# A constant deviation bound in place of a measured one, and pair differences on 32 rows, in a fused attention and MLP kernel

## The chip, the cores and the metric

The kernel runs on one core of a Trainium2 chip. The metric is the device time of one launch in microseconds (us); the time of a kernel is the median of its runs. The engines named are TensorE (PE, with its weight loads as PEld), VectorE (DVE), ScalarE (ACT), GpSimd (POOL) and SyncE (SP), whose queue issues the DMA transfers.

## The reference

Four batches of 12,480 rows of 128 numbers pass through two attention steps with 32 inducing points, and then through a two-layer MLP with a squared ReLU.

```python
x: (4, 12480, 128) float32, normal * 0.1      inducing: (32, 128) float32, normal * 0.1 * 2.776
w_in: (128, 2048), w_out: (2048, 128)

def mab(q, kv):
    s = scale * (q @ kv.transpose(0, 2, 1))
    s = s - s.max(-1, keepdims=True)
    a = np.exp(s)
    a /= a.sum(-1, keepdims=True) + 1e-09
    return a @ kv
h = mab(I, x)                  # 32 x 128 per batch
y = mab(x, h)                  # 12480 x 128 per batch
r = np.maximum(y @ w_in, 0.0)
out = (r * r) @ w_out
```

Each row of y is a weighted mean of the same 32 rows of h, with weights a that lie close to 1/32. The kernel uses this: y @ w_in is a @ (h @ w_in), so the MLP's first layer acts on 32 numbers in place of 128. Where a hidden column has one sign for all weights that can occur, its squared ReLU is zero or a plain square, and the sum over all such columns is a quadratic form in the 32 deviations d = 2^14 (a - 1/32). Only columns that may change sign are computed one by one; there is room for 16 of them per batch.

## The kernel before, in words

A batch has 26 chunks of 480 columns (4 groups of 120 rows). Chunks are grouped by four into 7 groups G. Four things are done for each batch.

`first(b)` (L238) computes the scores of the inducing points against x: it loads tiles `xp` (128 x 1920, nine buffers), multiplies (`scores`, L236), scales and takes the maximum on DVE (L254), exponentiates on ACT (L300), transposes on DVE (L310), and accumulates `hacc` on PE (L323) over blocks `xnb` of x (five buffers). It ends with `hT`, the 32 rows of h and their mean. `second(b, G)` multiplies the same xp tile with hT (freeing it), and forms the softmax over 32 in alternating steps on DVE, POOL and ACT. It writes the deviations as two fp16 halves, upper and lower, in the tile `a16`, to memory (`ad`, L389), and loads them back transposed as `dT` (L409): rows 0 to 31 the upper half, rows 32 to 63 the lower, rows 64 to 95 the upper again. `squares(b, G)` forms squares of the 16 single columns and of the mixed columns on PE, DVE and POOL, and puts them in rows 96 to 127 of dT. `prepare(b)` computes h @ w_in (`hwv`), decides which hidden columns are always off, always on or mixed, and makes the weights of the quadratic form: products `G` on DVE (L605), `wq` on PE (L611), then `w16` and `lin`.

For each chunk, `Chunk.up` makes two matmuls `hp` into two PSUM banks (L639), twice; their stationary operand `pairs` forms differences of two deviations, 512 of them in four blocks. `lift` squares two banks at once on ACT (L648). `down` sums four products with w16 and one with lin into `po` (L654, L655), which ACT or DVE scales (L658, L660), and SP stores.

Which columns count as mixed depends on rho, a bound on how far a weight can deviate from 1/32, relative to 1/32. Before the change it is measured: `largest(G)` (L290) takes the largest magnitude in every xp tile on DVE (`xm`, L292), `prepare` folds those with the spread of h (`dh`, L456 to L459), a matmul (L474) and a small row of two numbers, broadcast as `two` (L484).

```python
ts(row[:, 1:2], row[:, 1:2], 2 * scale * (1 + 2.0 ** -8), 2.0 ** -16, op0=ALU.mult, op1=ALU.add)
```

At the end `flags`, one number for each batch, tells whether the short way was allowed: rho small enough, at most 16 mixed columns, weights in range. If one is 0, the last part of the kernel (`every_column`) computes everything again by all 2,048 columns.

What runs beside what is fixed twice. The code interleaves the generators `first`, `prepare`, `second` and `squares` of the coming groups with the chunks (`background`, by counts of steps). The instructions so written are then put in an order for each engine by a simulated timeline, which uses its own estimates of durations and landings; an engine executes its own list strictly in order. A change of one instruction's cost can so move others. Besides, `held` sums expected work of ACT and DVE and gives some evacuations to the one with less.

Of the kernel before, what the change touches and what calls it, by code (L numbers as in the profile page):

```python
# [40 lines left out]
def attend_then_relu2_mlp(ctx: ExitStack, tc: tile.TileContext, xn, xT, indT, w_in, w_out, outT):  # L41
# [198 lines left out]
    def first(b):  # L240
# [49 lines left out]
        def largest(G):  # L290
            held["dve"] += 60 + 1.042 * 4 * WID[G]
            nc.vector.tensor_reduce(  # L292
                st.xm[:, G:G + 1], st.xp[G], axis=AX.X, op=ALU.max, apply_absolute_value=True,
            )

# [141 lines left out]
    def prepare(b):  # L437
# [37 lines left out]
        row = work.tile([1, 2], F32, tag="row", name=f"row_{b}")
        nc.vector.tensor_reduce(row[:, 0:1], ps[0:1, 0:P], axis=AX.X, op=ALU.max)
        nc.vector.tensor_reduce(row[:, 1:2], ps[0:1, P:P + MI], axis=AX.X, op=ALU.max)
        ts(row[:, 0:1], row[:, 0:1], 2.0 ** -60, None, op0=ALU.max)
        ts(row[:, 1:2], row[:, 1:2], 2 * scale * (1 + 2.0 ** -8), 2.0 ** -16, op0=ALU.mult, op1=ALU.add)
# [149 lines left out]
    class Chunk:  # L629
# [4 lines left out]
        def up(self, j):  # L634
            if j == 0:
                self.dT = self.st.aT[self.c // 4][:, :, (self.c % 4) * TP:(self.c % 4 + 1) * TP]
            hp = self.hp[j] = two_banks(f"hp_{self.b}_{self.c}_{j}")
            for i in range(2):
                nc.tensor.matmul(  # L639
                    hp[:, i, 0:CH].rearrange("p (q t) -> p q t", q=4), pairs[0:96, (2 * j + i) * P:(2 * j + i + 1) * P],  # L640
                    self.dT[0:96], start=True, stop=True,
                )
# [297 lines left out]
```

## Time and profile before

| | |
|---|---|
| three runs | 562.49, 556.12, 562.29 us; median 562.29 |
| profiled execution | 565.03 us, of which the span of instructions is 563.2 |
| granted TensorE clock, mean | 0.87 of full speed |
| DMA | 100.83 MB, mean 179 GB/s |
| first square of a chunk (ACT L648) | 96.3 us |
| first squares of batches 1, 2, 3 | 223.5, 350.7, 470.3 us |

The profile is read from several views: the busy time of each engine; the same cut into stages, with the columns PE, PEld, DVE, ACT, POOL, granted clock, DMA share and GB/s; groups of instructions by line with their busy time, the mean duration of one in ns, and the idle time ahead of them with what ended it; instructions in order of time; and the chain of waits, which is followed back from the last instruction of the span to what released it.

### The profile page before, as it was taken

Reading aid. Unit: us, or ns where it says so; the run is one execution under the profiler, and the core shown is the slowest. Engines: PE = TensorE matmul, PEld = TensorE weight load, DVE = VectorE, ACT = ScalarE, POOL = GpSimd, SP = SyncE. Lnnn points to the kernel's source line nnn. Section 1 sums busy time; section 2 is a strip of 40 time slices with the busy share of each in tenths; the row PEclk is TensorE's granted clock in tenths of the full one; section 3 lists DMA queues with packets and bytes.
Section 4 is the critical chain, followed back from the end, with each engine's and each line's share of the span. In section 5 each row is a group of like instructions: output and inputs, shape, how many; then the busy total and the mean of one; then the engine's idle time right before and its main releaser. Section 6 shows DMA issues by size and latency. Waiting matters only on the chain.

```text
span 563.2 us, 8828 instructions
## 1 busy us (share of the span) xinstructions
PE 422.6 (75%) x3083; PEld 202.7 (36%) x3083; DVE 365.6 (65%) x947; ACT 294.4 (52%) x419; POOL 82.2 (15%) x93
## 2 busy tenths in 40 slices
PE   1635355986778988869789889779779989669792
PEld 0023334622233535522244536423234555223340
DVE  8999768466382674675574384986653377787541
ACT  0030113338395794334687883426486875357771
POOL 0000011021120110122211010132121021234200
PEclk9999557699697998776899988878898999898987
DMA  8998313126559863253778943263567312244642
GB/s 317 410 358 310 132 70 118 41 80 212 140 160 345 292 216 115 72 169 107 216 237 294 334 167 115 76 227 115 174 216 264 128 54 72 90 151 133 203 150 82
DMA packets 64591, 100.83 MB, mean 179 GB/s; under 512 B 22800, under 2 KB 53776, under 8 KB 64528
## 3 DMA queue, kind: packets, MB, share of 16 engines
q1 hardware_dynamic: 64528, 100.08, 52.9%
q8 instruction: 28, 0.46, 0.4%
q14 instruction: 35, 0.29, 0.2%
HBM read 64.91 MB, written 31.95 MB: 172 GB/s over the span
## 4 chain that ended last, share of the span: by engine, by line
PE 39%; DMA 24%; DVE 22%; ACT 5%; SPq 4%; issue 3%; POOL 0%; ACTq 0%; DVEq 0%; POOLq 0%
PE hp L639 11%; DMA dT<-ad 7%; PE po L654 6%; PE s L236 6%; DMA xp_False<-xT_dram 6%; DMA ad<-a 5%; DVE xm L292 5%; ACT g L648 4%; DMA xnb<-xn_dram 3%; PE wq L611 3%; DVE G L605 3%; PE hwv L448 3%; PE hacc L323 2%; SPq L409 2%; DMA outT_dram<-o 2%
## 5 line engine op out<-in xcount | busy, mean ns | idle before, releaser
L648 ACT ACTIVATE g<-hp 128x960 f16<-128x960 f32 x208 | 193.5, 972 | 105.0 <-PE hp L639 92.8
L639 PE MATMUL hp<-dT,pairs 96*128 96x480 f16 x416 | 129.3, 407 | 16.2 <-ACT g L648 9.6
L654 PE MATMUL po<-g,w 128*128 128x480 f16 x416 | 114.7, 381 | 13.0 <-DVE o L660 5.1
L639 PEld LDWEIGHTS <-pairs 96*128 96x128 f16 x416 | 36.8, 104 | 84.4 <-issue 60.2
L368 POOL TENSOR_TENSOR e<-e,mx 128x480 f32<-128x480 f32 (+1 forms) x28 | 27.0, 965 | 261.5 <-DVE mx L364 208.2
L654 PEld LDWEIGHTS <-w 128*128 128x128 f16 x416 | 40.9, 102 | 63.6 <-issue 24.6
L292 DVE TENSOR_REDUCE xm<-xp_False 128x1 f32<-128x1920 f32 (+1 forms) x28 | 55.9, 1999 | 8.4 <-DMA xp_False<-xT_dram 8.3
L658 ACT ACTIVATE o<-po,bias,osc 128x480 f32<-128x480 f32 x66 | 48.7, 757 | 15.6 <-PE po L655 14.7
L236 PE MATMUL s<-xp_False,indT_sb 128*32 128x480 f32 (+1 forms) x224 | 37.4, 756 | 18.3 <-DMA xp_False<-xT_dram 13.3
L323 PE MATMUL hacc<-xnb,en 128*32 128x128 f32 x784 | 35.6, 317 | 19.6 <-DMA xnb<-xn_dram 7.6
L655 PE MATMUL po<-dT,lin 128*128 128x480 f16 x104 | 39.9, 400 | 9.3 <-DMA dT<-zz 9.0
L432 POOL TENSOR_TENSOR zz<-z 128x480 f16<-128x480 f32 (+1 forms) x28 | 27.6, 985 | 111.7 <-DVE z L428 87.9
L660 DVE TENSOR_SCALAR o<-po,osc,bias 128x480 f32<-128x480 f32 x38 | 28.8, 763 | 18.4 <-PE po L655 13.7
L375 POOL TENSOR_TENSOR e<-e,z 128x480 f32<-128x480 f32 (+1 forms) x28 | 26.9, 961 | 87.8 <-DVE z L374 67.6
L323 PEld LDWEIGHTS hacc<-xnb,en 128*32 128x32 f32 x784 | 25.5, 125 | 32.5 <-issue 15.7
L300 ACT ACTIVATE sT<-sT,nb 128x480 f32<-128x480 f32 (+1 forms) x28 | 18.3, 657 | 35.2 <-DVE nb L287 35.2
L362 DVE STREAM_TRANSPOSE e<-s 128x480 f32<-128x480 f32 (+1 forms) x28 | 18.0, 644 | 25.6 <-PE s L236 25.4
L428 DVE TENSOR_SCALAR z<-sq,off,cut 128x480 f32<-128x480 f32 (+1 forms) x28 | 21.5, 769 | 18.0 <-PE sq L422 17.5
L236 PE MATMUL s<-xp_False,hT 128*32 128x480 f32 (+1 forms) x224 | 30.0, 610 | 0.1
L605 DVE TENSOR_TENSOR G<-hwp,hw 128x512 f16<-128x512 f16 x64 | 25.9, 460 | 5.6 <-PE wq L611 5.6
L378 DVE STREAM_TRANSPOSE a<-e 128x480 f32<-128x480 f32 (+1 forms) x28 | 17.7, 633 | 13.0 <-POOL e L375 13.0
L422 PE MATMUL sq<-dT,singles 96*32 96x480 f16 x104 | 11.4, 398 | 19.4 <-DMA dT<-ad 18.0
(208 smaller groups left out, 493.3 us busy)
## 6 DMA issues: line engine op xcount, KB each, us to landing
outT_dram<-o SPq DMA_DIRECT2D x104, 240.0 KB, 2.6
xp_False<-xT_dram SPq DMA_DIRECT2D x24, 960.0 KB, 6.3
xnb<-xn_dram SPq DMA_DIRECT2D x28, 448.0 KB, 5.8
xnb<-xn_dram SPq DMA_DIRECT2D x24, 512.0 KB, 6.5
dT<-ad SPq DMA_DIRECT2D x72, 120.0 KB, 2.6
ad<-a SPq DMA_DIRECT2D x24, 240.0 KB, 2.6
dT<-zz SPq DMA_DIRECT2D x104, 30.0 KB, 1.9
wi<-w_in_dram SPq DMA_DIRECT2D x4, 512.0 KB, 5.7
```

What stands on the lines that cost most here:

```text
L236: nc.tensor.matmul(ps[32 * q:32 * q + 32, 0:w], lhsT, xp[:, w * q:w * q + w], start=True, stop=True,)
L292: nc.vector.tensor_reduce(st.xm[:, G:G + 1], st.xp[G], axis=AX.X, op=ALU.max, apply_absolute_value=True,)
L323: st.last = nc.tensor.matmul(hacc[32 * q:32 * q + 32, 0:P], en[:, t], xg[:, t % 8], start=t < 4, stop=t + 4 >= nb32,)
L368: nc.gpsimd.tensor_tensor(e[:, 0:t], e[:, 0:t], mx[:, 0:t].unsqueeze(2).broadcast_to([P, t, MI]), op=ALU.subtract)
L432: nc.gpsimd.tensor_tensor(g[rows], zv[rows], zv[rows], op=ALU.mult)
L605: tt(g[:, :, MI * j:MI * j + n], hwp[:, :, 0:n], hw16f[:, :, s0:s0 + n], op=ALU.mult)
L639: nc.tensor.matmul(hp[:, i, 0:CH].rearrange("p (q t) -> p q t", q=4), pairs[0:96, (2 * j + i) * P:(2 * j + i + 1) * P], self.dT[0:96], sta ...
L648: nc.scalar.activation(self.g[:, 2 * j:2 * j + 2], self.hp.pop(j)[:, 0:2, 0:CH], AF.Square)
L654: nc.tensor.matmul(po[:, 0:CH], st.w16[:, i], self.g[:, i], start=i == 0, stop=False)
L655: nc.tensor.matmul(po[:, 0:CH].rearrange("p (q t) -> p q t", q=4), st.lin, self.dT, start=False, stop=True)
L658: nc.scalar.activation(o, po[:, 0:CH], AF.Identity, bias=st.bias, scale=st.osc)
L660: nc.vector.tensor_scalar(o, po[:, 0:CH], st.osc, st.bias, op0=ALU.mult, op1=ALU.add)
```

## The change

rho becomes the constant 2^-10, and the measured bound goes. In its place, after the deviations of a group are written as fp16, DVE folds their upper half into a running minimum `least_d`; after the last group, `smallest` reduces it to one number and sets a fifth flag if it is at least -0.498 (that is, if no weight fell more than about 2^-10, relative, below 1/32). The pair differences are formed from the upper half alone: each of the two matmuls of a pair reads 32 rows of `pairs` and dT, the first rows 0 to 31, the second rows 64 to 95, where both formerly read rows 0 to 95 (upper half, lower half, zeros). The loads of dT are unchanged. The lower half of the deviations so no longer enters the pair differences; it still enters the linear part and the squares.

```diff
-RHO_MAX = 2.0 ** -8
+RHO = 2.0 ** -10
+D_MIN = -0.498
...
+    def half_rows(block):
+        return slice(64, 96) if block % 2 else slice(0, 32)
+
     for s in range(1, 17):
         n = MI if s < 16 else 16
+        r = half_rows((s - 1) // 4)
         nc.vector.tensor_tensor(
-            pairs[0:64, MI * (s - 1):MI * (s - 1) + n], fold_f[0:64, 0:n], fold_f[0:64, s:s + n], op=ALU.subtract,
+            pairs[r, MI * (s - 1):MI * (s - 1) + n], fold_f[r, 0:n], fold_f[r, s:s + n], op=ALU.subtract,
         )
...
-        def largest(G):
-            held["dve"] += 60 + 1.042 * 4 * WID[G]
-            nc.vector.tensor_reduce(
-                st.xm[:, G:G + 1], st.xp[G], axis=AX.X, op=ALU.max, apply_absolute_value=True,
-            )
-
...
-            largest(G)
...
         if not again:
+            nc.vector.tensor_tensor(least_d[:, 0:w], least_d[:, 0:w], a16[:, 0, 0:w], op=ALU.min)
             st.aT[G] = load_dT(b, G)
...
-                xm, dh, ah = small("xm"), small("dh", MI), small("ah", MI)
-                nc.vector.tensor_reduce(xm, st.xm, axis=AX.X, op=ALU.max)
-                ts(dh, st.hT[:, 0:MI], st.hT[:, P:P + 1], None, op0=ALU.subtract)
-                stt(dh, dh, -1.0, dh, op0=ALU.mult, op1=ALU.max)
-                stt(ah, st.hT[:, 0:MI], -1.0, st.hT[:, 0:MI], op0=ALU.mult, op1=ALU.max)
-                stt(dh, ah, 2.0 ** -18, dh, op0=ALU.mult, op1=ALU.add)
...
-        nc.tensor.matmul(ps[0:1, P:P + MI], xm, dh, start=True, stop=True)
...
-        nc.tensor.matmul(ps[:, 0:2], ones, row, start=True, stop=True)
-        two = small("two", 2)
-        nc.vector.tensor_copy(two, ps[:, 0:2])
-        rho = two[:, 1:2]
+        nc.tensor.matmul(ps[:, 0:1], ones, row, start=True, stop=True)
...
-        ts(vm, v, omr, None, op0=ALU.mult)
-        ts(up, hi, 0.0, rho, op0=ALU.max, op1=ALU.mult)
+        ts(vm, v, 1.0 - RHO, None, op0=ALU.mult)
+        ts(up, hi, 0.0, RHO, op0=ALU.max, op1=ALU.mult)
...
-        fits = work.tile([1, 2], F32, tag="fits", name=f"fits_{b}")
-        ts(fits[:, 0:1], bp[0:1, 2:3], MX + 0.5, None, op0=ALU.is_le)
-        ts(fits[:, 1:2], row[:, 1:2], RHO_MAX, None, op0=ALU.is_le)
-        tt(flags[:, b:b + 1], fits[:, 0:1], fits[:, 1:2], op=ALU.mult)
+        ts(flags[:, b:b + 1], bp[0:1, 2:3], MX + 0.5, None, op0=ALU.is_le)
...
             for i in range(2):
+                r = half_rows(i)
                 nc.tensor.matmul(
-                    hp[:, i, 0:CH].rearrange("p (q t) -> p q t", q=4), pairs[0:96, (2 * j + i) * P:(2 * j + i + 1) * P],
-                    self.dT[0:96], start=True, stop=True,
+                    hp[:, i, 0:CH].rearrange("p (q t) -> p q t", q=4), pairs[r, (2 * j + i) * P:(2 * j + i + 1) * P],
+                    self.dT[r], start=True, stop=True,
                 )
...
+    def smallest():
+
+        m = small("dmin")
+        nc.vector.tensor_reduce(m, least_d, axis=AX.X, op=ALU.min)
+        tp = att_psum("dmin_t")
+        nc.tensor.transpose(tp[0:1, 0:P], m, ident)
+        t = work.tile([1, 1], F32, tag="dmin1", name="dmin1")
+        nc.vector.tensor_reduce(t, tp[0:1, 0:P], axis=AX.X, op=ALU.min)
+        nc.vector.tensor_scalar(flags[:, NB:NB + 1], t, D_MIN, None, op0=ALU.is_ge)
+        yield
+
+    ahead = chain(*(second(b, G) for b in range(NB) for G in range(NG)), smallest())
```

The order of the engines changes with it. On DVE in the first microseconds, where w_in is narrowed from 64-bit words (`ni`, `w_in_sb`) while the first scores arrive (`s1`, scaled into `sT`), the list before is:

```order
L292 TENSOR_REDUCE xm0_133<-xp_0_0_False_179 128x1
L210 TENSOR_TENSOR ni1_r_205<-ni1_a_203,ni1_r_205 128x512
L211 TENSOR_SCALAR ni1_m_204<-wi1_173 128x512
L254 TENSOR_SCALAR sT_0_213,mx_0_215<-s1_0_0_216 128x480
L292 TENSOR_REDUCE xm0_133<-xp_0_1_False_181 128x1
L206 TENSOR_SCALAR ni2_a_222<-wi2_175 128x512
L212 SCALAR_TENSOR_TENSOR w_in_sb_128<-ni1_m_204,ni1_r_205 128x512
L254 TENSOR_SCALAR sT_0_213,mx_0_215<-s1_0_1_232 128x480
```

The list of the changed kernel at the same place, whose lines stand a few lines further down in its own file, is:

```order
L218 TENSOR_TENSOR ni1_r_205<-ni1_a_203,ni1_r_205 128x512
L219 TENSOR_SCALAR ni1_m_204<-wi1_173 128x512
L214 TENSOR_SCALAR ni2_a_222<-wi2_175 128x512
L220 SCALAR_TENSOR_TENSOR w_in_sb_128<-ni1_m_204,ni1_r_205 128x512
L262 TENSOR_SCALAR sT_0_213,mx_0_215<-s1_0_0_216 128x480
L215 SCALAR_TENSOR_TENSOR ni2_a_222<-wi2_175,ni2_a_222 128x512
L216 TENSOR_SCALAR ni2_m_223<-ni2_a_222 128x512
L217 SCALAR_TENSOR_TENSOR ni2_r_224<-wi2_175,ni2_m_223 128x512
L262 TENSOR_SCALAR sT_0_213,mx_0_215<-s1_0_1_232 128x480
```

The maxima are gone, and the narrowing of w_in and then of w_out moves ahead, between and before the scores; the narrowing of w_out, which ended behind batch 0's hT, now ends by the fourth of the seven `hacc` sums.

On DVE at the start of batch 0's `prepare`, a maximum over a tile of batch 1 stands ahead of the extremes `hi_c` and `lo_c` of h @ w_in:

```order
L372 TENSOR_REDUCE z2_0_0_582<-e2_0_0_557 128x15
L292 TENSOR_REDUCE xm1_144<-xp_1_2_False_984 128x1
L463 TENSOR_REDUCE hi_c_573<-hwv_0_533 128x16
L464 TENSOR_REDUCE lo_c_574<-hwv_0_533 128x16
L373 TENSOR_SCALAR z2_0_0_582<-z2_0_0_582 128x15
```

In the changed kernel the extremes follow at once, and the products with the now constant rho stand ahead of the maximum `am2`:

```order
L373 TENSOR_REDUCE z2_0_0_567<-e2_0_0_542 128x15
L457 TENSOR_REDUCE hi_c_558<-hwv_0_526 128x16
L458 TENSOR_REDUCE lo_c_559<-hwv_0_526 128x16
L374 TENSOR_SCALAR z2_0_0_567<-z2_0_0_567 128x15
L491 TENSOR_SCALAR vm_620<-hwv_0_526 128x16
L461 TENSOR_REDUCE am2_563<-hi_c_558 128x1
L492 TENSOR_SCALAR up_c_614<-hi_c_558 128x16
```

On DVE in batch 1's `prepare`, where the weights of the quadratic form begin, a maximum over a tile of batch 2 stands ahead of `hwS` and `G`:

```order
L521 TENSOR_TENSOR mix_1707<-pos_1706,dead_1705 128x16
L525 TENSOR_TENSOR hwp_1_1745<-hw16_1_1697,pos_1706 128x512
L292 TENSOR_REDUCE xm0_133<-xp_2_2_False_2290 128x1
L520 TENSOR_TENSOR hwS_1_1740<-hws_1_1695,sum_c_1737 128x512
L522 TENSOR_SCALAR mix_1707<-mix_1707 128x16
L605 TENSOR_TENSOR G_1_0_1919<-hwp_1_1745,hw16_1_1697 128x16x32 x4
```

In the changed kernel nothing of batch 2 stands there, an evacuation of `squares` (`z`) has come in, and G stands ahead of hwS:

```order
L508 TENSOR_TENSOR mix_1667<-pos_1666,dead_1665 128x16
L512 TENSOR_TENSOR hwp_1_1705<-hw16_1_1658,pos_1666 128x512
L430 TENSOR_SCALAR z_0_5_1685<-sq_0_5_1680,off0_138,cut_102 128x480
L505 TENSOR_TENSOR sum_c_1697<-sum_c_1697,pos_1666 128x16
L509 TENSOR_SCALAR mix_1667<-mix_1667 128x16
L589 TENSOR_TENSOR G_1_0_1877<-hwp_1_1705,hw16_1_1658 128x16x32 x4
L507 TENSOR_TENSOR hwS_1_1700<-hws_1_1656,sum_c_1697 128x512
```

On PE the matmuls keep their order in the main, but the groups of consecutive hp matmuls become 177 where they were 160.

More of the change, by code (lines that the diff above doesn't have):

```diff
@@ L108, in attend_then_relu2_mlp @@
     fold_f = fold.rearrange("p k i -> p (k i)")
+    def half_rows(block):
+        return slice(64, 96) if block % 2 else slice(0, 32)
     for s in range(1, 17):
         n = MI if s < 16 else 16
+        r = half_rows((s - 1) // 4)
         nc.vector.tensor_tensor(
-            pairs[0:64, MI * (s - 1):MI * (s - 1) + n], fold_f[0:64, 0:n], fold_f[0:64, s:s + n], op=ALU.subtract,
+            pairs[r, MI * (s - 1):MI * (s - 1) + n], fold_f[r, 0:n], fold_f[r, s:s + n], op=ALU.subtract,
         )
-    nc.vector.tensor_copy(pairs[0:64, 31 * 16:32 * 16], fold_f[0:64, 0:16])
+    r = half_rows(NQ - 1)
+    nc.vector.tensor_copy(pairs[r, 31 * 16:32 * 16], fold_f[r, 0:16])
     w_in_sb = const.tile([P, NF * P], F32, name="w_in_sb")
@@ L119, in attend_then_relu2_mlp @@
     inv_t = const.tile([P, 1], F32, name="inv_t")
-    flags = const.tile([1, NB], F32, name="flags")
+    flags = const.tile([1, NB + 1], F32, name="flags")
+    least_d = const.tile([P, CH], F16, name="least_d")
+    nc.vector.memset(least_d, 0.0)
     class Batch:
@@ L127, in attend_then_relu2_mlp @@
         one = Batch()
-        one.xm = const.tile([P, NG], F32, name=f"xm{k}")
         one.hn = const.tile([P, P], F32, name=f"hn{k}")
@@ L451, in prepare @@
             evac(hwv[:, 8 * h:8 * h + 8].rearrange("p k i -> p (k i)"), ps[:, 0:8 * (MI + 1)], 8 * (MI + 1))
-            if h == 0:
-                xm, dh, ah = small("xm"), small("dh", MI), small("ah", MI)
-                nc.vector.tensor_reduce(xm, st.xm, axis=AX.X, op=ALU.max)
-                ts(dh, st.hT[:, 0:MI], st.hT[:, P:P + 1], None, op0=ALU.subtract)
-                stt(dh, dh, -1.0, dh, op0=ALU.mult, op1=ALU.max)
-                stt(ah, st.hT[:, 0:MI], -1.0, st.hT[:, 0:MI], op0=ALU.mult, op1=ALU.max)
-                stt(dh, ah, 2.0 ** -18, dh, op0=ALU.mult, op1=ALU.add)
             yield
@@ L473, in prepare @@
         nc.tensor.transpose(ps[0:1, 0:P], am, ident)
-        nc.tensor.matmul(ps[0:1, P:P + MI], xm, dh, start=True, stop=True)
[L475 to L479, printed above, removed]
+        row = work.tile([1, 1], F32, tag="row", name=f"row_{b}")
+        nc.vector.tensor_reduce(row, ps[0:1, 0:P], axis=AX.X, op=ALU.max)
+        ts(row, row, 2.0 ** -60, None, op0=ALU.max)
         yield
         ps = att_psum(f"bc_{b}")
-        nc.tensor.matmul(ps[:, 0:2], ones, row, start=True, stop=True)
-        two = small("two", 2)
-        nc.vector.tensor_copy(two, ps[:, 0:2])
-        rho = two[:, 1:2]
+        nc.tensor.matmul(ps[:, 0:1], ones, row, start=True, stop=True)
         p2 = small("p2")
-        ts(p2.bitcast(I32), two[:, 0:1].bitcast(I32), 0x7F800000, None, op0=ALU.bitwise_and)
-        mg, nmg, s, k2, omr = small("mg"), small("nmg"), small("s"), small("k2"), small("omr")
+        ts(p2.bitcast(I32), ps[:, 0:1].bitcast(I32), 0x7F800000, None, op0=ALU.bitwise_and)
+        mg, nmg, s, k2 = small("mg"), small("nmg"), small("s"), small("k2")
         ts(k2, p2, 2.0, None, op0=ALU.mult)
@@ L500, in prepare @@
         ts(nmg, p2, -2.0 ** -16, None, op0=ALU.mult)
-        ts(omr, rho, -1.0, 1.0, op0=ALU.mult, op1=ALU.add)
         up, dn, dead, pos, mix, inc = (small(n, NF) for n in ("up_c", "dn_c", "dead", "pos", "mix", "inc"))
         vm = small("vm", NF)
-        ts(vm, v, omr, None, op0=ALU.mult)
-        ts(up, hi, 0.0, rho, op0=ALU.max, op1=ALU.mult)
+        ts(vm, v, 1.0 - RHO, None, op0=ALU.mult)
+        ts(up, hi, 0.0, RHO, op0=ALU.max, op1=ALU.mult)
         tt(up, up, vm, op=ALU.add)
@@ L508, in prepare @@
         stt(dead, up, nmg, dead, op0=ALU.is_le, op1=ALU.max)
-        ts(dn, lo, 0.0, rho, op0=ALU.min, op1=ALU.mult)
+        ts(dn, lo, 0.0, RHO, op0=ALU.min, op1=ALU.mult)
         tt(dn, dn, vm, op=ALU.add)
@@ L703, in attend_then_relu2_mlp @@
     N_SECOND, N_SCORES, N_HEADS, N_PRE, N_SQ = 4, 2 * NG, 20, 23, 2
-    ahead = chain(*(second(b, G) for b in range(NB) for G in range(NG)))
+    def smallest():
[8 more added lines that the diff above has]
+    ahead = chain(*(second(b, G) for b in range(NB) for G in range(NG)), smallest())
     sqs = chain(*(squares(b, G) for b in range(NB) for G in range(NG)))
@@ L723, in background @@
         b, c = k // (2 * NCH), k % (2 * NCH) / 2.0
-        give("ahead", ahead, min(math.ceil((NG * b + c / 4 + min(3, 2 + k / 16)) * N_SECOND), NB * NG * N_SECOND))
+        give("ahead", ahead, min(math.ceil((NG * b + c / 4 + min(3, 2 + k / 16)) * N_SECOND), NB * NG * N_SECOND + 1))
         if b + 1 < NB:
```

## The prediction

> **What bounds the kernel now.** I read the page's busy shares and its chain first, then the span cut into stages, then the groups of instructions, and last the places where the chain meets the changed lines.
>
> ```profile
> PE 422.6 (75%) x3083; PEld 202.7 (36%) x3083; DVE 365.6 (65%) x947; ACT 294.4 (52%) x419; POOL 82.2 (15%) x93
> PE 39%; DMA 24%; DVE 22%; ACT 5%; SPq 4%; issue 3%; POOL 0%; ACTq 0%; DVEq 0%; POOLq 0%
> 0.00:96.00 96.00, 43.48 (x352) 24.55 (x352) 82.61 (x214) 12.40 (x25) 5.15 (x13) 0.82 0.68 251
> 96.00:223.00 127.00, 103.08 (x796) 50.00 (x795) 72.87 (x209) 77.78 (x114) 16.95 (x18) 0.87 0.55 178
> 470.00:563.00 93.00, 68.12 (x378) 28.97 (x375) 57.57 (x116) 53.44 (x64) 19.57 (x20) 0.91 0.38 123
> ```
>
> No engine is full over the span, so the average decides nothing. In the first row by stages (columns PE, PEld, DVE, ACT, POOL, clock, DMA share, GB/s) DVE is busy 83 of 96 us before the first square of a chunk. In the stage of batch 0 it is 73 of 127 and PE 103 of 127. There the chain runs through PE, DMA round trips and an in-order DVE.
>
> ```profile
> L292 DVE TENSOR_REDUCE xm<-xp_False 128x1 f32<-128x1920 f32 (+1 forms) x28 | 55.9, 1999 | 8.4 <-DMA xp_False<-xT_dram 8.3
> 0.00:64.00 64.00, 18.20 (x9) 0.95 0.89 336
> 64.00:96.00 32.00, 4.30 (x2) 0.56 0.26 81
> 96.00:223.00 127.00, 11.90 (x6) 0.87 0.55 178
> 223.00:350.00 127.00, 13.97 (x7) 0.84 0.57 188
> 350.00:470.00 120.00, 7.53 (x4) 0.90 0.48 157
> ```
>
> This is the instruction that the change removes: 28 maxima over a whole xp tile, 55.9 us of DVE, some 2 us each. By the rows for this line alone 18.2 us lie in the first 64, 4.3 until 96, 33.4 (11.9 + 14.0 + 7.5) in the stages of batches 0 to 2, none in batch 3.
>
> **The start.**
>
> ```profile
> 12.23 2.15 DVE L292 TENSOR_REDUCE xm<-xp_False 128x1 f32<-128x1920 f32 x1 [1.23 <-DMA xp_False<-xT_dram]
> 0.00:4.00 4.00, 0.00 (x0) 0.00 (x0) 3.18 (x33) 1.28 (x1) 1.18 (x9) 1.00 0.45 129
> 4.00:40.00 36.00, 13.81 (x79) 2.96 (x83) 34.00 (x62) 2.81 (x9) 0.00 (x0) 1.00 1.03 402
> 40.00:56.00 16.00, 9.81 (x184) 7.41 (x176) 15.93 (x31) 1.85 (x7) 0.00 (x0) 1.00 0.84 283
> 56.00:64.00 8.00, 1.25 (x3) 0.69 (x3) 7.93 (x23) 0.00 (x0) 0.00 (x0) 0.63 0.62 247
> 55.31 0.64 PE L323 MATMUL hacc<-xnb,en 128*32 128x128 f32 x16 [0.65 <-DMA xnb<-xn_dram]
> 67.23 3.62 PE L448 MATMUL hwv<-hT,w_in_sb 128*128 128x33 f32 x16
> ```
>
> From 12 to 64 us DVE never rests, and nine maxima are 18.2 of those us. Without them DVE's work ends near 64 - 18 = 46. DMA is the next limit: full at 402 GB/s until 40 us, then only 283 since the xnb buffers wait for hacc. Up to 56 us it moved 0.5 + 14.5 + 4.5 = 19.5 MB (rate times length of each row, the first 4 us at 129 GB/s). At 402 GB/s throughout that is 4 + 19.0/0.402 = 51 us; the last block that hacc needs comes shortly before, near 50. So hacc ends near 50.5 instead of 55.9. From there the old order needs 11.3 us to hwv, since DVE still narrows w_out; now w_out is narrowed ahead of the last hacc sums, and what is left (hq, hs, zr, hn, ht, hT, wo_m, wo_b) is some 4. First hwv at 54.5: **-12.8 us**. Ends: -9, if DMA slows under new collisions, and -18.
>
> **Batch 0's preparation.**
>
> ```profile
> 76.21 0.38 ACT L163 COPY hwv<-hwv 128x264 f32<-128x264 f32 x1 [0.44 <-PE hwv L448]
> 77.10 2.15 DVE L292 TENSOR_REDUCE xm<-xp_False 128x1 f32<-128x1920 f32 x1 [0.64 <-DMA xp_False<-xT_dram]
> 79.17 0.68 DVE L463 TENSOR_REDUCE hi_c<-hwv 128x16 f32<-128x512 f32 x1
> 82.06 0.14 DVE L478 TENSOR_SCALAR row<-row 1x1 f32<-1x1 f32 x1
> 96.34 2.67 ACT L648 ACTIVATE g<-hp 128x960 f16<-128x960 f32 x3
> ```
>
> hi_c needs only the copy that ends at 76.6, but stands behind a maximum of batch 1's tile. It starts 2.6 us sooner. Eleven small operations per batch go too (dh, ah, the second row, two, omr, fits); at 0.14 each with their spacing of 0.1, and one small matmul, that is about 1 us a batch. Here 0.5 of it counts: **-3.1 us**. The SP queue's order hardly changes: the next xp load still stands ahead of the first ad store, and both move up with the scores that free the tile.
>
> **Batches 0 to 2.** The chain meets maxima here:
>
> ```profile
> 207.09 0.68 DVE L525 TENSOR_TENSOR hwp<-hw,pos 128x512 f16<-128x512 f16 x1
> 207.86 2.15 DVE L292 TENSOR_REDUCE xm<-xp_False 128x1 f32<-128x1920 f32 x1
> 209.93 0.68 DVE L520 TENSOR_TENSOR hwS<-hws,sum_c 128x512 f32<-128x512 f32 x1
> 135.04 0.83 DVE xm L292
> 153.43 1.15 DVE xm L292
> 207.90 2.03 issue
> 238.39 2.06 DVE xm L292
> 290.52 1.65 issue
> 361.36 2.06 DVE xm L292
> ```
>
> The maximum of xp_2_2 stands ahead of batch 1's hwS and G, on which the next w16 depends. The chain's piece called issue at 207.90 is that same maximum. Pieces of this line between 96 and 470 are 0.83 + 1.15 + 2.06 + 2.06 = 6.1, and 2.03 + 1.65 under issue, 9.8 in all. The other 23.6 us and the 8.3 us of DVE idle ahead of maxima are hidden now behind PE and DMA trips; a little comes out. I take **-12 us**; ends 0 (each time a DMA trip ends as late anyway) and -33. What is late next is PE, or the trip a to ad to dT.
>
> **PE.** The pair differences go from one 96-row operand to two 32-row operands on different rows. The row groups that the trace has are column groups:
>
> ```profile
> 305.88 0.58 PE L639 MATMUL hp<-dT,pairs 96*128 96x480 f16 x2
> 306.29 0.57 PE L654 MATMUL po<-g,w 128*128 128x480 f16 x2
> 306.79 0.39 PE L422 MATMUL sq<-dT,singles 96*32 96x480 f16 x4
> 307.11 0.58 PE L639 MATMUL hp<-dT,pairs 96*128 96x480 f16 x2
> L639 PEld LDWEIGHTS <-pairs x416: 95/98/259, 95.1 to 549.9; 96*128 96x128 f16 x139
> ```
>
> Two hp take 306.29 - 305.88 = 0.41, 0.205 each. Four sq on four column groups take 0.39 together, so they run side by side. But entering that shape costs 306.79 - 306.29 - 0.41 = 0.09, and leaving it 307.11 - 306.79 - 0.205 = 0.115, about a weight load of 98 ns. If row groups behave like this, 208 pairs save 208 x 0.205 = 42.6, and a lone pair between two po gives it all back: 0.205 saved, 0.205 for the two shape changes. In the new program's order 101 groups of hp follow a full-size matmul and 157 are followed by one: 101 x 0.09 + 157 x 0.115 = 27.2. PE's issue time falls by 15.4 of 422.6. At PE's 39% of the chain: **-6 us**. Ends: -15.4, and +27.2 if the pairs don't run side by side.
>
> The Trainium skill, page TensorE: Matmul & The Clock Gate, section Part 3, says that matmuls on distinct row groups overlap with starts some 4 ns apart, and gives 3.07x for four. By that alone the term would be 0.39 x 42.6 = 16.6 us of gain. The page TensorEngine Tiling (Array Packing), Key Properties, says that a change of tiling mode drains the engine. The 0.09 and 0.115 around sq agree; no row here shows row groups.
>
> **What is added.**
>
> ```profile
> L605 DVE TENSOR_TENSOR G<-hwp,hw 128x512 f16<-128x512 f16 x60 | 25.1, 473 | 5.6 <-PE wq L611 5.6
> L236 PE MATMUL s<-xp_False,hT x224: 363/566/1010, 70.8 to 515.5; 128*32 128x480 f32 x96, 128*32 128x240 f32 x16
> ```
>
> 28 minima of f16 tiles into least_d, priced by this f16 operation of two inputs: 24 x 473 x 480/512 ns and four half as wide make 11.5 us. Nothing on another engine waits for them, but a16's successor on DVE does; at DVE's 22% of the chain **+2.5 us**, ends 0 and 11.5. The other three batches' small operations give **-2 us** (half of some 1.3 each; ends 0 and -4). The final minimum over least_d follows the last score group, whose matmuls start until 515.5 of 563.2: some 40 us of chunks cover it, 0; with that cover gone about 1.5 (an estimate: six operations of the size of row's and am's). pairs and flags at the start and end: under 0.5. DMA bytes don't change.
>
> **Sum.** 565.03 for the profiled execution (its span 563.2 and 1.8 around it) - 12.8 - 3.1 - 12 - 6 + 2.5 - 2 = 531.6. The median of the three runs is 562.29, 0.5% below the profiled one, so **529 us**.
>
> **Rivals.**
> 1. DVE is what paces the batches after all: all 33.4 us come out, 21 more than taken, 508 us. For it: every store ad passes through four DVE operations in a row. Against: DVE's 57% share there. Chance 0.14.
> 2. Only the start and the preparation gain, and each later stall is taken over by a DMA trip or by PE: 565 - 15.9 + 0.5 = 549.6, 547 us. For it: batch 3, without any maximum, still takes 93 us. Chance 0.17.
> 3. The pairs run one after the other: 0.39 x 27.2 = +10.6 instead of -6, 546 us. Chance 0.06.
> 4. Less PE work lets the clock fall. It stood at 0.50 in this stage:
>
> ```profile
> 64.00:84.00 20.00, 11.94 (x56) 8.62 (x56) 10.82 (x43) 4.06 (x5) 1.99 (x2) 0.50 0.14 50
> ```
>
> From 0.87 to 0.80 PE's part of the chain, 0.39 x 563 = 220 us, would grow by 9%: +19, 548 us. Against it: hp's stages stay densely fed. Chance 0.05. The Trainium skill, TensorE: Matmul & The Clock Gate, Part 1, describes a clock halved after an idle window; the 0.50 here agrees.
>
> 5. Slower: each of the 416 hp exposes its own weight load of 98 ns, and none run side by side. PE gains 40.8 + 27.2 = 68 us of work and becomes the bound: 531.6 + 6 + 68 = 606, 603 us. It decides against the change from some 40 us more of PE, 0.19 us per pair. Against it: the four sq loads show no such thing. Chance 0.05, with the small remainder that the new constant bound is not met and all is computed again; from the reference's formulas and inputs the smallest deviation is -0.064 against -0.498, so it should be.
>
> **Numbers.** The forecast has 0.53. The range of 508 to 549 takes in rivals 1 to 4 and leaves out the slower one and the tails of the others. Faster by over 2% (about what a measurement of this kernel can tell from no change) means below 551: the forecast, rival 1, and some two thirds of rivals 2 to 4, 0.86. Within 2%: 0.09. Slower: 0.05.
>
> **What would show it.** The first hwv near 54.5 us instead of 67.2, with DMA full until some 50; the first square near 80 instead of 96.3 (the row of g above); no DVE idle on xp ahead of hi_c; batches 0 to 2 some 6 us shorter each; two hp starting within 10 ns, a matmul of another shape behind them some 0.1 us late; DVE busy near 318 us. The prediction falls if the stages after 96 us don't shrink (rival 2), or if hp pairs start 0.2 us apart (3 and 5).

## The result: 529.4 us, and where the time went

| | before | changed |
|---|---|---|
| median | 562.39 us (556.12 to 564.34, 4 runs) | 529.43 us (526.49 to 535.06, 4 runs) |
| ratio, 95% interval | | 0.9415 (0.931 to 0.9519) |
| profiled execution, its span | 565.03, 563.2 | 530.98, 529.1 |
| first hwv | 67.2 us | 55.8 us |
| first squares of batches 0 to 3 | 96.3, 223.5, 350.7, 470.3 | 82.2, 200.5, 324.2, 435.6 |
| length of batches 0 to 3 | 127.2, 127.2, 119.6, 92.9 | 118.3, 123.7, 111.4, 93.5 |

The total is the forecast one. Medians and ranges are of all runs, while the ratios with their intervals leave out runs over 1.5% longer than the fastest of the same kernel. The page of the changed kernel, with busy time, chain, granted clock and DMA share:

```profile
PE 411.5 (78%) x3076; PEld 176.5 (33%) x3076; DVE 344.3 (65%) x941; ACT 275.1 (52%) x385; POOL 83.6 (16%) x93
PEclk9876659999867879787979788859969789887997
DMA  8999531167499523366699733465594030355542
PE 41%; DMA 24%; DVE 16%; issue 8%; ACT 7%; SPq 2%; POOL 1%; ACTq 0%; DVEq 0%; POOLq 0%
```

Two of these numbers aren't as forecast. DVE is busy 344 us, not some 318, although all 55.9 us of maxima are gone. And the whole span's granted clock fell from 0.87 to 0.83.

The long pieces of the changed kernel's chain at the start (start, us, piece):

```profile
9.46 16.75 DMA wo<-w_out_dram
...
34.33 10.08 DMA xnb<-xn_dram
...
46.74 4.93 DMA xnb<-xn_dram
55.85 3.56 PE hwv L450 x16
```

Its windows there (columns as in the forecast):

```profile
4.00:40.00 36.00, 14.97 (x135) 5.62 (x135) 33.16 (x83) 4.66 (x14) 0.00 (x0) 0.84 1.03 405
40.00:56.00 16.00, 8.61 (x127) 5.23 (x128) 11.58 (x32) 0.00 (x0) 0.00 (x0) 0.71 1.00 373
```

And its PE in order of time, the last hacc and the first hwv:

```profile
51.80 0.64 PE L324 MATMUL hacc<-xnb,en 128*32 128x128 f32 x16 [0.59 <-DMA xnb<-xn_dram]
55.78 3.63 PE L450 MATMUL hwv<-hT,w_in_sb 128*128 128x33 f32 x16
```

From 40 to 56 us DVE, which never rested here before, is busy 11.6 of 16 us, and DMA stays full (share 1.00, 373 GB/s) where it was at 283 GB/s. The long pieces of the chain at the start are three loads and then hwv: DMA is the next limit. It is a little slower than the 402 GB/s that I had reckoned with to the end, so the last hacc starts at 51.8 and hwv at 55.8. The rest of the span cut at the first squares:

```profile
0.00:82.00 82.00, 40.96 (x352) 23.57 (x353) 64.52 (x198) 12.84 (x25) 5.36 (x13) 0.73 0.78 294
82.00:200.50 118.50, 97.12 (x786) 42.37 (x783) 60.08 (x186) 76.50 (x112) 17.71 (x18) 0.87 0.58 188
200.50:324.00 123.50, 107.11 (x816) 47.30 (x814) 82.33 (x230) 67.14 (x96) 20.63 (x21) 0.84 0.61 197
324.00:435.50 111.50, 95.85 (x726) 39.52 (x725) 74.09 (x190) 65.54 (x92) 20.39 (x21) 0.83 0.51 163
435.50:529.00 93.50, 70.50 (x405) 23.70 (x403) 63.23 (x138) 53.09 (x62) 19.50 (x20) 0.88 0.39 127
```

Of the 34.1 us of span, 14.1 come out ahead of the first square and 20.0 behind it. In batch 1, DVE (third busy column) has 82.3 us of work, more than the 76.0 of before, in a stage that lost its maxima. The groups of the page show what came in, for PE's pairs and the evacuations `o` on DVE and on ACT:

```profile
L624 PE MATMUL hp<-dT,pairs 32*128 32x480 f16 x416 | 86.8, 405 | 21.6 <-ACT g L633 11.6
L645 DVE TENSOR_SCALAR o<-po,osc,bias 128x480 f32<-128x480 f32 x64 | 49.1, 767 | 37.9 <-PE po L640 26.9
L643 ACT ACTIVATE o<-po,bias,osc 128x480 f32<-128x480 f32 x40 | 29.9, 759 | 10.6 <-PE po L640 10.5
```

The same page of the kernel before has for `o`:

```profile
L658 ACT ACTIVATE o<-po,bias,osc 128x480 f32<-128x480 f32 x66 | 48.7, 757 | 15.6 <-PE po L655 14.7
...
L660 DVE TENSOR_SCALAR o<-po,osc,bias 128x480 f32<-128x480 f32 x38 | 28.8, 763 | 18.4 <-PE po L655 13.7
```

26 of 104 evacuations, 20 us, moved from ACT to DVE, and so did six of the `lessen` steps that choose their engine by the same sum. `largest` held not only the maximum but the line that entered its 2 us in `held["dve"]`. Without that line DVE looks less loaded by the planner's sum, and gets more.

The pairs run side by side, as PE in order of time shows:

```profile
124.53 0.37 PE L624 MATMUL hp<-dT,pairs 32*128 32x480 f16 x2
124.84 0.58 PE L639 MATMUL po<-g,w 128*128 128x480 f16 x2
125.35 0.38 PE L624 MATMUL hp<-dT,pairs 32*128 32x480 f16 x2
125.65 0.58 PE L639 MATMUL po<-g,w 128*128 128x480 f16 x2
126.48 0.36 PE L640 MATMUL po<-dT,lin 128*128 128x480 f16 x1 [0.25 <-DMA dT<-zz]
```

Two hp take 0.37 us together, as one `po` alone does; in the single records they start 3 ns apart (median of the 208 pairs). From the start of the pair to `po` it is 0.31 us, 0.205 for the pair and 0.10 for the change of shape; from `po` to the next pair 0.51, two times 0.205 and 0.10.

### The profile page after: what moved, and what is told of

It is laid out like the page before. It is cut to its first block, busy times and chain, and to the rows that moved or that the text cites. A ratio compares the mean times of both kernels' runs of the same rounds, so it can differ in the third digit from the quotient of the medians.

```text
span 529.1 us, 8779 instructions
## 1 busy us (share of the span) xinstructions
PE 411.5 (78%) x3076; PEld 176.5 (33%) x3076; DVE 344.3 (65%) x941; ACT 275.1 (52%) x385; POOL 83.6 (16%) x93
## 3 DMA queue, kind: packets, MB, share of 16 engines
q1 hardware_dynamic: 64528, 100.08, 56.5%
## 4 chain that ended last, share of the span: by engine, by line
PE 41%; DMA 24%; DVE 16%; issue 8%; ACT 7%; SPq 2%; POOL 1%; ACTq 0%; DVEq 0%; POOLq 0%
PE po L639 12%; PE hp L624 7%; DMA xnb<-xn_dram 7%; PE s L244 5%; DMA dT<-ad 4%; ACT g L633 4%; DVE G L589 4%; PE hwv L450 3%; DMA ad<-a 3%; DMA wo<-w_out_dram 3%; PE hacc L324 3%; PE po L640 3%; PE R L516 2%; DMA dT<-zz 2%; DMA xp_False<-xT_dram 2%
## 5 line engine op out<-in xcount | busy, mean ns | idle before, releaser
L639 PE MATMUL po<-g,w 128*128 128x480 f16 x416 | 125.8, 406 | 7.6 <-ACT o L643 3.0
L624 PE MATMUL hp<-dT,pairs 32*128 32x480 f16 x416 | 86.8, 405 | 21.6 <-ACT g L633 11.6
L645 DVE TENSOR_SCALAR o<-po,osc,bias 128x480 f32<-128x480 f32 x64 | 49.1, 767 | 37.9 <-PE po L640 26.9
L624 PEld LDWEIGHTS <-pairs 32*128 32x128 f16 x416 | 20.9, 94 | 101.2 <-issue 86.2
L639 PEld LDWEIGHTS <-w 128*128 128x128 f16 x416 | 31.1, 102 | 64.9 <-issue 52.0
L643 ACT ACTIVATE o<-po,bias,osc 128x480 f32<-128x480 f32 x40 | 29.9, 759 | 10.6 <-PE po L640 10.5
L589 DVE TENSOR_TENSOR G<-hwp,hw 128x512 f16<-128x512 f16 x64 | 30.4, 532 | 3.6 <-PE wq L595 3.6
L370 ACT ACTIVATE e<-e 128x480 f32<-128x480 f32 (+1 forms) x28 | 16.1, 576 | 25.3 <-POOL e L369 25.2
L516 PE MATMUL R<-wo_sb,hwS 128*32 128x128 f32 x128 | 22.4, 357 | 8.4 <-DVE hwS L507 8.4
L595 PE MATMUL wq<-w_hi,G 128*128 128x128 f16 x256 | 20.7, 246 | 8.0 <-DVE z L430 2.8
```

Source lines behind the costliest of these rows:

```text
L516: nc.tensor.matmul(ps[0:MI, 0:P], hwS[:, k], wo_sb[:, k], start=k == 0, stop=k == NF - 1)
L589: tt(g[:, :, MI * j:MI * j + n], hwp[:, :, 0:n], hw16f[:, :, s0:s0 + n], op=ALU.mult)
L624: nc.tensor.matmul(hp[:, i, 0:CH].rearrange("p (q t) -> p q t", q=4), pairs[r, (2 * j + i) * P:(2 * j + i + 1) * P], self.dT[r], start=Tru ...
L639: nc.tensor.matmul(po[:, 0:CH], st.w16[:, i], self.g[:, i], start=i == 0, stop=False)
L643: nc.scalar.activation(o, po[:, 0:CH], AF.Identity, bias=st.bias, scale=st.osc)
L645: nc.vector.tensor_scalar(o, po[:, 0:CH], st.osc, st.bias, op0=ALU.mult, op1=ALU.add)
```

## Experiments

All kernels, with the time of the kernel before in the same comparison. A dash stands where there is no interval. Clock is the mean of the whole-span clocks of all runs; the columns behind it are of one profiled execution.

| kernel | median us (range) | before | ratio, 95% | clock | first square | batches 0 to 3 | DVE busy |
|---|---|---|---|---|---|---|---|
| e1, pairs on 96 rows | 525.48 (519.09 to 529.0) | 560.34 | 0.9378 (0.9197 to 0.956) | 0.887 | 83.6 | 122.8, 119.5, 108.9, 90.4 | 344.3 |
| e2, kernel before with 32-row pairs | 550.66 (539.32 to 556.14) | 560.34 | - | 0.824 | 96.0 | 127.5, 122.5, 118.1, 86.1 | 366.6 |
| e3, old split | 528.13 (526.52 to 529.36) | 560.34 | 0.9495 (0.9385 to 0.9604) | 0.844 | 83.1 | 122.5, 112.9, 111.5, 96.2 | 324.6 |
| e4, both halves on the same rows | 552.55 (546.07 to 570.44) | 560.34 | 0.9867 (0.9675 to 1.006) | 0.830 | 83.5 | 137.8, 119.0, 114.3, 97.3 | 347.3 |
| e5, no least_d | 532.73 (525.8 to 536.24) | 558.95 | - | 0.841 | 83.4 | 123.3, 111.3, 119.3, 91.2 | 333.0 |
| e6, maxima in batches 1 to 3 | 563.5 (555.5 to 565.9) | 558.95 | 1.0087 (1.0006 to 1.0168) | 0.818 | 86.7 | 141.2, 125.6, 114.1, 94.8 | 377.2 |
| e7, maxima in batch 0 | 533.33 (528.82 to 543.33) | 558.95 | 0.9495 (0.9405 to 0.9585) | 0.851 | 88.7 | 118.8, 117.7, 114.2, 92.3 | 357.0 |
| f1, changed kernel again | 532.25 (527.25 to 544.56) | 558.17 | 0.9474 (0.9403 to 0.9546) | 0.841 | 83.3 | 117.2, 122.9, 107.2, 96.2 | 343.6 |
| f2, 96 rows again | 525.24 (520.0 to 532.37) | 558.17 | 0.9405 (0.9345 to 0.9464) | 0.889 | 83.8 | 120.2, 113.7, 111.9, 90.6 | 343.5 |
| f3, 96 rows and old split | 510.81 (508.14 to 512.98) | 558.17 | 0.9159 (0.9112 to 0.9206) | 0.896 | 83.7 | 118.6, 110.4, 106.1, 90.7 | 321.7 |
| g1, f3 with maxima in batches 1 to 3 | 529.55 (528.06 to 533.65) | 561.93 | 0.9444 (0.9374 to 0.9514) | 0.875 | 87.5 | 130.2, 110.8, 111.3, 87.6 | 361.4 |
| g2, f3 with extra changes of shape | 532.91 (530.73 to 537.24) | 561.93 | 0.9512 (0.9446 to 0.9579) | 0.893 | 82.4 | 130.8, 113.9, 109.1, 92.8 | 320.9 |

### The two parts alone

e1 is the changed kernel with each pair's matmul again over 96 rows; e2 is the kernel before, with only the 32-row pairs put in.

```diff
-                    hp[:, i, 0:CH]..., pairs[r, (2 * j + i) * P:(2 * j + i + 1) * P],
-                    self.dT[r], start=True, stop=True,
+                    hp[:, i, 0:CH]..., pairs[0:96, (2 * j + i) * P:(2 * j + i + 1) * P],
+                    self.dT[0:96], start=True, stop=True,
```

> The changed kernel with the pair differences taken back to 96 rows, so the constant bound, the minimum and the dropped maxima alone. Theory (the maxima on DVE carry most of the change, the 32-row pairs some 6 us): about 535 us, a ratio of 0.95 to before; hp starts 0.2 us apart again. Rival (the pairs running side by side carry the gain): 550 to 562 us. Second rival (the pairs give nothing, since shape changes eat all of it): 529 us or less.

> The kernel before with the 32-row pairs alone; the maxima stay. Theory: PE issues some 15 us less, 6 us of which come out: about 556 us, ratio 0.99. Rival (pairs carry the gain): 530 to 540 us. Rival (shape changes eat it, or the clock falls with PE's load): 562 us or more.

The bound alone is as fast as the whole change, if not faster: 525.5 beside 529.4, with intervals that overlap; the theory's 535 was 10 us too high. So the pairs didn't give their 6 us there. Put into the kernel before they show a median 10 us lower, but over runs that spread by 17 us and without an interval; that doesn't settle it. What e1 does show is the clock, 0.887 over its runs with 96 rows.

### The evacuations' split

e3 is the changed kernel with the entry in the planner's sum kept, and nothing computed for it.

```diff
+            held["dve"] += 60 + 1.042 * 4 * WID[G]
```

> The changed kernel with one line kept: the expected 2 us of each dropped maximum are still added to DVE's account, so that 66 of the 104 output evacuations go to ACT as before the change, where the changed kernel gives ACT 40 (and 19 of 28 lessened a, where it gives 13). Theory (the shift put some 26 x 0.77 us back on DVE and is why DVE fell by 21 us and not by 48): DVE busy near 320 us, time 523 to 528 us. Rival (ACT and its squares are what the chunks wait for, so DVE is the better place for them): 530 to 538 us.

The split comes back (66 on ACT, 38 on DVE), DVE falls by 20 us to 324.6, near the forecast 318, and the time stays within the spread of the changed kernel: its median is 1 to 4 us below the two medians of the changed kernel (529.4 and 532.3), its ratio 0.002 to 0.008 above theirs. With 32-row pairs DVE's extra 20 us cost nothing that these runs can tell.

### Side by side, or on the same rows

e4 puts both of a pair's blocks on rows 0 to 31, so that they can't overlap. All else, the order and the number of shape changes too, is that of the changed kernel.

```diff
     def half_rows(block):
-        return slice(64, 96) if block % 2 else slice(0, 32)
+        return slice(0, 32)
```

> The changed kernel with both matmuls of a pair on rows 0 to 31, so each still has the 32-row shape but they share a row group. Theory: hp pairs start 0.2 us apart, the entry and exit stay 0.1 us each, PE has 43 us more to issue than the changed kernel, and at PE's 0.4 of the chain the time is 540 to 548 us. Rival (PE has slack in the stages, which wait for DMA and DVE): within 3 us of the changed kernel, 527 to 532 us.

In e4's PE in order of time the pair takes 0.57 us, and the changes of shape stay, 0.51 from pair to `po` as two times 0.205 and 0.10:

```profile
129.54 0.57 PE L624 MATMUL hp<-dT,pairs 32*128 32x480 f16 x2
130.05 0.58 PE L639 MATMUL po<-g,w 128*128 128x480 f16 x2
130.46 0.37 PE L640 MATMUL po<-dT,lin 128*128 128x480 f16 x1
```

It is 20 to 23 us slower than the changed kernel. So running side by side is worth that much, once the shape changes are paid for; the kernels with 96 rows neither pay the one nor get the other. e4 also has a busier PE, and not the clock of e1. The whole-span row of e1 (windows; columns as above):

```profile
0.00:525.00 525.00, 407.36 (x3076) 199.42 (x3076) 344.26 (x941) 274.25 (x385) 82.87 (x93) 0.88 0.58 192
```

And that of e4:

```profile
0.00:551.90 551.90, 453.01 (x3076) 190.17 (x3076) 347.31 (x941) 278.29 (x385) 83.69 (x93) 0.83 0.55 183
```

PE is busy 453 of 552 us in e4, 82%, against 78% in e1, at 0.83 against 0.88. It is not even over the span, though: by stages e4 had 0.78 in batch 0 and 0.93 in batch 2.

### The minimum

e5 leaves out the minima into least_d, so that the fifth flag is always 1.

```diff
-            nc.vector.tensor_tensor(least_d[:, 0:w], least_d[:, 0:w], a16[:, 0, 0:w], op=ALU.min)
```

> The changed kernel without the 28 running minima into least_d; the tile stays zero, so the fifth flag is always 1 and the guard on the deviations is left out. Theory (13.9 us of DVE, of which its share of the chain comes out): 2 to 4 us faster than the changed kernel, 525 to 528 us. Rival (the guard hides in DVE's idle time): no difference, 529 us.

DVE has 11 us less to do, and the time shows no gain: 532.7 beside 529.4 and 532.3 of the changed kernel in other comparisons. The minima are hidden, or worth less than the some 10 us by which single runs differ.

### The maxima put back

e6 and e7 add the maxima to the changed kernel, for batches 1 to 3 and for batch 0; the values go into a tile that nothing reads, and the planner's sum doesn't count them.

```diff
+            if b:
+                nc.vector.tensor_reduce(
+                    st.xm[:, G:G + 1], st.xp[G], axis=AX.X, op=ALU.max, apply_absolute_value=True,
+                )
```

(e7 has `if b == 0:`.)

> The changed kernel with the maxima over xp put back for batches 1 to 3 (21 of 28); their results are not used. Theory (the maxima stand in DVE's order ahead of the next weights and cost the batches some 12 us, and 2 to 4 us in the start, where the order puts two of them): 540 to 547 us; first hwv near 58 us. Rival (batches wait for PE and DMA, the maxima there are hidden): 529 to 533 us.

> The changed kernel with the maxima over xp put back for batch 0 alone (7 of 28); their results are not used. Theory (DVE bounds the start): first hwv 8 to 11 us later, near 65 us, and the time 537 to 541 us. Rival (DMA bounds the start as much, so the 13.5 us hide behind the loads): first hwv before 59 us, time 529 to 533 us.

With batch 0's seven maxima back, hwv goes from 55.8 to 62.7 us and the first square from 82.2 to 88.7; the total moves by 1 to 4 us, so both expectations were off: DVE held up the start, but part of what it loses is regained behind it. With the other 21 back the whole gain is gone, 563.5 us, 31 to 34 more, where the theory had at most 547. These 21 maxima last 42.1 us, 33.5 of them in the stages of batches 0 to 2. But e6 has the new split as well, on a DVE now busy 377 us, and the 32-row pairs. So the price had to be taken again without both, in g1.

### The corners of pairs and split

f1 is the changed kernel and f2 is e1, both again; f3 is e1 with the planner's entry kept, as in e3. These three ran on one chip; e3, the fourth corner, ran on another, so its ratio is the safer figure.

> The changed kernel itself, for a comparison in one call with the two that follow: 526 to 533 us, mean clock near 0.84.

> The constant bound with 96-row pairs once more, beside the changed kernel. Theory (32-row pairs save PE issue time, but the granted clock falls from about 0.88 to 0.84 and takes it back): 2 to 6 us faster than the changed kernel, clock 0.87 to 0.90. Rival (the 4 us seen between them were the spread of runs): within 2 us.

> 96-row pairs, constant bound, and the old split of evacuations between ACT and DVE. Theory (the two edits are independent; the split alone was worth 1 us): 522 to 527 us. Rival (ACT's longer share delays the squares): 528 to 533 us.

f3 is the fastest of all, 510.8 us, 0.9159 of the kernel before (0.9112 to 0.9206), below what either expectation had, and beats the changed kernel by 21 us (18 by the ratios). The two parts work on each other: with 96-row pairs the new split costs 14.4 us (f2 against f3, intervals apart); with 32-row pairs little or nothing. And with the old split the 32-row pairs cost 17 us (e3 against f3, intervals apart; 19 by the ratios); with the new one 4 to 7, within overlapping intervals. The stages of f3:

```profile
0.00:83.50 83.50, 42.14 (x351) 23.77 (x352) 64.00 (x198) 12.84 (x25) 5.35 (x13) 0.75 0.78 290
83.50:202.50 119.00, 100.35 (x840) 50.32 (x839) 64.61 (x210) 78.19 (x115) 17.36 (x18) 0.96 0.59 188
202.50:312.50 110.00, 93.46 (x764) 45.07 (x763) 65.52 (x193) 78.08 (x113) 20.48 (x21) 0.94 0.67 220
312.50:419.00 106.50, 93.42 (x752) 45.16 (x751) 67.29 (x186) 72.38 (x105) 20.41 (x21) 0.95 0.55 174
419.00:509.50 90.50, 66.30 (x376) 29.43 (x374) 60.26 (x123) 53.59 (x64) 19.68 (x20) 0.88 0.39 126
```

Beside the stages of the changed kernel: in batch 1 DVE has 65.5 us in place of 82.3, and the clock is 0.94 to 0.96 in batches 0 to 2, where it was 0.83 to 0.87. Batch 1 is 13 us shorter. That stage alone doesn't show the gain, though: e3 and e5, no faster than the changed kernel, have batches 1 of 112.9 and 111.3 us too, and lose it in others.

### The maxima's price without the new split

g1 is f3 with the maxima of e6 and the planner's entry for them.

> The kernel with 96-row pairs, constant bound and the old split (511 us), with the maxima over xp put back for batches 1 to 3; their results are not used. It tells the maxima's price in the batches from that of the split, which the run with maxima and the new split mixed. Theory (their price in the batches is about what the prediction took, 12 us, and some 4 in the start): 523 to 530 us. Rival (nearly all of the 42 us of 21 maxima comes out): 540 to 553 us.

21 maxima cost 18.7 us beside f3 by the medians, 16 by the ratios (g1 and f3 ran on two chips): 3.8 ahead of the first square by the profiles, and so 12 to 15 behind it. They stand on g1's chain so:

```profile
40.31 2.06 DVE xm L320
...
67.44 2.15 DVE xm L320
...
140.85 1.15 DVE xm L320
...
176.93 2.06 DVE xm L320
...
220.41 2.03 issue
```

The piece called issue is a maximum too: DVE ran one from 220.38 to 222.53. The pieces at 140.85 and 176.93 lie in batch 0's stage, which is also where the time is (118.6 to 130.2); they make 3.2 of its 11.6 us, and the rest isn't on the chain as maxima. The stages of batches 1 to 3 differ by +0.4, +5.2 and -3.1. But g1 is still 32 us faster than the kernel before, with the maxima of three batches back. Of that, the start explains some 9. Batches 1 and 2 of the kernel before (windows):

```profile
223.50:350.70 127.20, 106.52 (x772) 51.01 (x770) 75.99 (x201) 78.64 (x113) 20.31 (x21) 0.85 0.57 190
350.70:470.30 119.60, 101.24 (x794) 48.16 (x793) 76.83 (x211) 72.13 (x104) 20.21 (x21) 0.90 0.48 156
```

And of g1:

```profile
217.70:328.50 110.80, 96.61 (x754) 44.81 (x753) 77.01 (x197) 77.47 (x113) 19.94 (x21) 0.92 0.66 215
328.50:439.80 111.30, 93.69 (x746) 44.67 (x745) 75.81 (x190) 72.29 (x103) 21.07 (x21) 0.92 0.52 168
```

DVE and ACT do the same work in the same stage, which is 16 us shorter in batch 1. Some 10 of these are PE's busy time at a clock of 0.92 in place of 0.85, the other 6 its idle time. What is left different in this stage is the small operations of the measured bound, the seven minima that came in for them, and the order that the simulated timeline made. Which of them it is wasn't tried apart.

### What a change of shape costs

g2 is f3 with one matmul of 32 rows and one column behind each pair, into a column that nothing reads. PE so changes shape about as often as in the changed kernel, with pairs of 96 rows and none side by side.

```diff
+            nc.tensor.matmul(hp[:, 1, CH:CH + 1], pairs[0:32, 0:P], self.dT[0:32, 0, 0:1], start=True, stop=True)
```

> The same 511 us kernel with one more tiny matmul behind each pair: 32 rows, one column, into a PSUM column that nothing reads, so that PE changes shape as often as with 32-row pairs, while the pairs keep their 96 rows. Theory (the clock falls because the pairs fill fewer rows of the array): clock stays at 0.88 to 0.90; PE pays the shape changes, some 0.2 us x 208 at 0.4 of the chain, 525 to 535 us. Rival (the gaps of the shape changes lower the clock): clock 0.83 to 0.85, and 540 us or more.

PE of g2 in order of time:

```profile
129.88 0.58 PE L624 MATMUL hp<-dT,pairs 96*128 96x480 f16 x2
130.39 0.17 PE L628 MATMUL hp<-dT,pairs 32*128 32x1 f16 x1
130.50 0.58 PE L624 MATMUL hp<-dT,pairs 96*128 96x480 f16 x2
131.01 0.17 PE L628 MATMUL hp<-dT,pairs 32*128 32x1 f16 x1
131.11 1.01 PE L244 MATMUL s<-xp_False,hT 128*32 128x480 f32 x8
```

The tiny one starts 0.51 us behind the pair, 0.10 more than two times 0.205, and the next starts 0.11 behind it. So a change in and out is 0.2 us for a matmul of hardly any length. 208 of them make 43 us of PE's time, and the kernel is 22 us slower than f3 (20 by the ratios): about half of it is on the path. The clock stays at 0.893. The gaps of changing shape so aren't what lowers the clock in the 32-row kernels.

## Why the prediction came out, step by step

The total was right, 529 against 529.4; its terms weren't all, and that it came within 1 us is luck, as the ladder below shows.

**The start.** Forecast first hwv 54.5 (-12.8), measured 55.8 (-11.4): DVE was what was in the way, and DMA is the next limit, as f1 to f3 show again (hwv at 56.9, 56.1, 56.5). e7 is the counter-test. Seven maxima of 14.0 us in all move hwv by 6.9 us, and only 1 to 4 us of that reach the end of the span.

**Batch 0's preparation.** -3.1 forecast, -2.7 measured (first square 82.2, 26.4 us behind hwv where it was 29.1). The first square was to be near 80 and missed by the start's 1.3 and some of its own.

**Batches 0 to 2.** "Some 6 us shorter each": 8.9, 3.5 and 8.2. The maxima were priced at -12 of at most -33; g1 gives 12 to 15 behind the first square. The size holds, within what the runs can tell. The mechanism, an in-order DVE on which a hoisted maximum stands ahead of what PE waits for, is seen for 5.2 us of it, the three pieces behind the first square on g1's chain; for the rest it is argued. That all 33.4 come out (rival 1) is what e6 would suggest by itself; g1 shows that e6's price had a second cause in it, the new split, the 32-row pairs or both. That nothing comes out (rival 2) is excluded by g1's interval beside f3's.

**PE.** This is the step that failed. "PE's issue time falls by 15.4 of 422.6", -6 us at PE's share of the chain: the shapes behave as forecast (3 ns apart, 0.10 in and 0.10 out), so rival 3 is out, but the pairs cost 4 to 7 us in the changed kernel (within overlapping intervals) and 17 with the old split (clear of them). What was left out is the granted clock, which I had only as a rival of its own. Pages of e1 and of the changed kernel: hp falls from 121.3 to 86.8 us, a saving of 34.5; all other matmuls rise from 286.1 to 324.7. If busy time goes as one over the clock, 286.1 at e1's 0.879 becomes 301.9 at the changed kernel's 0.833; by this reckoning some 16 us of the rise are the clock, and the other 23 are about the 27 that I had counted for the changes of shape. Together they outweigh the saving. By the forecast's own arithmetic on the runs' clocks (0.889 to 0.841, 5.7% of a chain in which PE has 41% of 529) the clock costs 12 us, which with -6 makes +6. For the 17 us with the old split the same sum gives +7, and 10 stay without an explanation. This price of the clock is a sum: no run changed the clock alone, and e2, at 0.824 against 0.866, has a median below the kernel before and not above it.

Why the clock is lower stays open. Three pairs of kernels that differ in the rows alone, 96 and 32, have it lower by 0.04 to 0.05 (the kernel before 0.866, e2 0.824; f2 0.889, f1 0.841; f3 0.896, e3 0.844). Part of e2's fall lies in the start, where no pair runs (0.66 up to its first square, against 0.82). But batch by batch, too, the profiles of the kernel before, e1, f2 and f3 all have a higher clock than their partners with 32 rows (e2, the changed kernel, f1 and e3), by 0.02 to 0.12. It isn't the gaps (g2), nor does a busier PE bring it back (e4). Nor do 96 rows make a high clock by themselves: in batches 0 to 2 the kernel before has 0.85 to 0.90 with them, g1 0.91 to 0.92. That pairs which fill fewer rows count as less activity would fit most of this, but no run measured it apart from the kernel, and e4's batches 2 and 3 at 0.93 and 0.90 don't fit it well. The Trainium skill, page TensorE: Matmul & The Clock Gate, Part 1, has the gate follow how busy PE has been. The share of busy time in a profile doesn't order the clocks here: e4 has 82% at 0.83, e1 78% at 0.88.

**least_d.** 11.5 us of DVE forecast, 13.9 measured in the trace's groups of DVE's lines (28 at 497 ns; 11.5 in e1); +2.5 on the path is neither confirmed nor refuted by e5.

**The small operations** (-2) weren't tried by themselves.

**What no step had.** The diff shows the line `held["dve"] += ...` going, and I read over it as part of the maximum. It moved 20 us of evacuations to DVE and costs 14.4 us where the rest of the kernel is fast. And the kernel before is some 23 us slower behind its first square than g1 by the medians (27 by the stages of the two profiles), though g1 does nearly the same work; no step had this either. A ladder by ratios shows how the total came right: the kernel before 1, g1 0.944, f3 0.916 without the maxima, f2 0.941 with the new split, f1 0.947 with the 32-row pairs. One unforeseen gain (those 23 to 27 us) and two unforeseen losses (14.4 us by the split, and pairs that cost 4 to 7 us where 6 were to be gained) nearly cancel.

**Rivals 4 and 5.** The clock did fall, from 0.866 to 0.841 in the mean of runs, so rival 4's falling clock is there beside the forecast's terms, if not its 548 us. Its reason, less PE work, is not: PE is busy 78% of the span where it was 75%. Exposed weight loads (rival 5) are not: 0.51 us from a pair's `po` to the next pair is accounted for by the work and the change of shape.

**Open.** Which part of the order or of the small operations makes g1 faster than the kernel before, the largest piece of the whole gain; what lowers the clock; the 10 us above; and the luck of an order. Batch 3, whose work hardly differs between these kernels, lasts from 86.1 to 97.3 us among them, and batches 1 and 2 of e5 and of the changed kernel differ by -12.4 and +7.9 us at the same total, so a difference of some us in one stage of two profiles says little.

## What to carry to other kernels

When work goes out, look for the accounts that it was entered in: a balance between engines, a due time, an order that is computed from them; each is an edit of its own, to be tried by itself. Putting two small matmuls side by side pays only if enough of them follow each other to pay for the two changes of shape, and the clock that PE is then granted has to be counted too. A total that comes out as forecast proves none of its terms: here the best of four corners was some 20 us below the one that was forecast right.
